# Three visits of P.V instead of two in the first three heads of a fused attention and GLU kernel

## The chip, the cores and the metric

The kernel runs on one core of a Trainium2 chip. The metric is the time of one execution on the device in microseconds (us), median of several runs. The kernel before takes 2607.92 us (three runs, 2605.91 to 2611.41).

## The reference

One sequence of 2048 tokens, width 576, 32 heads of 18 columns, and a gated feed-forward of width 4608, all in float32. Both halves read the same normalised input, and their results are multiplied.

```python
xn = _layernorm(x, axis=-1)
qkv = xn @ wqkv                                  # 576 -> 3 * 576
p = _softmax(einsum("bhqd,bhkd->bhqk", q, k) * (Dh ** -0.5))
s = einsum("bhqk,bhkd->bhqd", p, v) @ wo
h = einsum("bsd,df->bsf", xn, w_gate) * einsum("bsd,df->bsf", xn, w_up)
g = _silu(einsum("bsf,fd->bsd", h, w_down))
return x + s * g
```

## The kernel before, in words

There are three stages. First come the layer norm, the q, k and v projections and the first loads of the feed-forward's weights. The main stage then does the whole attention and the whole feed-forward together. A short end stage applies wo, multiplies and adds. Products keep float32 accuracy by splitting operands into a high and a low part, so a matmul of the feed-forward comes in three terms.

In the main stage TensorE (PE) is split into two halves of 64 rows each. Each half takes matmuls of its own, side by side with the other's. Five kinds of work are dealt to them:

- **A items** (`a_item`, L655): scores of 128 queries against 512 keys, only to find each row's maximum. They run on half 0 (head 0's on both). VectorE (DVE) reduces each (L657). 64 per head.
- **B items** (`b_item`, L707): the scores once more, transposed and with the maximum subtracted. They run on half 1. ScalarE (ACT) takes the exponential (L709) into a buffer `pt`. 64 per head, four for each block `t` of 128 keys; the ring of `pt` holds eight such blocks.
- **The up and gate products** (`gu_op`, L760): up on half 0, gate on half 1, 27 matmuls of 512 columns for each block of 128 hidden columns. ACT, DVE and GpSimd (POOL) evacuate and split the product.
- **The down product** (`down_op`, L811): groups of twelve matmuls of 288 columns, six on half 0 and then six on half 1 in the same PSUM bank. DVE adds the sum to its accumulator (L874), or ACT copies it out (L868) and POOL adds it (L838).
- **P.V** (`pv_group`, L718): probabilities times values. It is the one kind that uses all 128 rows, split into four column blocks of 32. It can therefore only run when both halves are through with what they were given. Such a turn is called a **visit**. ACT copies out the sum of a head's first visit (L722), and DVE adds the sum of each later one (L724).

No engine decides this order while it runs. The kernel writes it when it is built: `order` keeps a planned clock for each half and for the other engines, and at each step takes the next A or B item, the next feed-forward matmul, or a visit. A and B items are paced by a course (`a_goal`, `b_goal`) that is renewed every 32 items from the work that is left (`keep_course`). A visit is wanted when enough finished blocks are due, and it waits until the two planned clocks stand within 0.04 us of each other, or 2 us have passed (L1274 to L1281). How many blocks are enough is what `wanted` says. It shares what is left of a head evenly among the fewest visits of at most `MANY` = 8 blocks: 16 blocks make two visits of eight. Once all B items are done, one block is enough.

Weights are loaded by SP. In the first of four passes over the tokens they come from the inputs (`wraw`, `draw`), are split by ACT and POOL (L255, L256, L293, L294), used, and stored to `swg` and `swd` (L264, L301); the later passes load the split form back (L246, L285). SP also loads the stacks of q and k for the coming head (`load_stack`, L321). SP's queue stands in the order that the plan's times gave.

Of the kernel before, what the change touches and what calls it, by code (L numbers as in the profile page):

```python
# [41 lines left out]
def kernel(  # L42
# [594 lines left out]
    with ExitStack() as mid:  # L637
# [373 lines left out]
        LEAD, MOST, MANY = 16, 40, 8  # L1011
# [17 lines left out]
        due, jobs, rows_done = [], [], {}  # L1029
# [148 lines left out]
        def wanted():  # L1178

            if not due:  # L1180
                return 0
            if nb == TOTAL:
                return 1
            left = NT - due[0][1]
            return left // -(-left // MANY)

        upped, gated, downed = {}, {}, {}

# [67 lines left out]
        def order():  # L1256
# [5 lines left out]
            while going(0) or going(1) or na < TOTAL or nb < TOTAL or due or jobs or soon or pool_later:  # L1262
# [7 lines left out]
                if job and max(next_free("a"), next_free("b")) <= min(clk):  # L1270
                    rows(job)
                    continue
                need = wanted() if next_free("g") < 1e9 else 0
                if (need and len(due) >= need and due[need - 1][2] <= now  # L1274
                        or any(j[1] is finish for j in jobs) and nb == TOTAL and not due):
# [175 lines left out]
```

## Time and profile before

| | |
|---|---|
| median of three runs | 2607.92 us |
| the profiled execution, its own time | 2609.18 us |
| its span in the trace | 2606.7 us |
| first stage (to the first A item, at 195.63) | 195.6 us |
| main stage (to the end stage's first transpose, at 2534.15) | 2338.5 us |
| of it P.V, 64 visits of 7.07 us | 452.7 us |
| end stage | 72.5 us |
| PE, DVE, ACT, POOL busy, share of the span | 99%, 68%, 60%, 26% |

A row of the grouped view reads: source line, engine, operation, tile written <- tiles read, shape, count, then busy time, mean ns of one, and the engine's idle time ahead of these instructions with what ended it. PE's busy time is the union of both halves: PE counts as busy while one half works alone. In the timeline a row is a start, a duration, and the instructions merged into it; a matmul's duration is the time through the array, and the spacing of starts is what it costs its half.

### The profile page before, as it was taken

To read this page: it belongs to the slowest core of one execution; us is meant where nothing else is said; L and a number is where in the kernel's file an instruction comes from. 1 tells how busy PE (TensorE), PEld (TensorE's weight loads), DVE (VectorE), ACT (ScalarE), POOL (GpSimd) and SP (SyncE) were. 2 spreads that over 40 slices of the span, in tenths; PEclk is the share of its full clock that TensorE was granted. 3 is DMA by queue.
4 is the path that set the end of the run, shared out by engine and by line. 5 is a ranking of instruction groups with operands and counts; after the bars stand their busy time and mean duration, and the time that the engine had idled before them with its cause. 6 is when DMAs were issued, how large, how long until landed. Compare 5 with 4: busy or idle time off the path is not lost.

```text
span 2606.7 us, 59535 instructions
## 1 busy us (share of the span) xinstructions
PE 2593.6 (99%) x24504; PEld 2136.3 (82%) x24504; DVE 1774.3 (68%) x2950; ACT 1560.1 (60%) x3122; POOL 678.6 (26%) x704
## 2 busy tenths in 40 slices
PE   8999999999999999999999999999999999999999
PEld 7899878878887878878877887887878877888799
DVE  7208666767777777767777877776778777776136
ACT  4223666667766666766666666666666666667512
POOL 3114434434431222222211222212111222212015
PEclk9999999999999999999999999999999999999999
DMA  7799767676653445445545444443453354433266
GB/s 247 240 291 265 201 186 189 182 192 191 176 185 118 141 137 179 151 144 170 144 167 150 142 143 131 135 140 134 147 174 111 135 153 149 143 117 126 96 242 214
DMA packets 207696, 435.11 MB, mean 167 GB/s; under 512 B 83168, under 2 KB 132992, under 8 KB 177216
## 3 DMA queue, kind: packets, MB, share of 16 engines
q1 hardware_dynamic: 205264, 423.35, 53.1%
q0 software_dynamic: 2160, 7.96, 0.8%
q8 instruction: 192, 3.15, 0.5%
q14 instruction: 80, 0.66, 0.1%
HBM read 314.64 MB, written 111.35 MB: 163 GB/s over the span
## 4 chain that ended last, share of the span: by engine, by line
PE 99%; DVE 0%; DMA 0%; ACT 0%; issue 0%; DVEq 0%
PE pg L760 35%; PE pg L718 17%; PE pg L811 16%; PE pa L655 11%; PE pb L707 9%; PE pb L447 2%; PE pg L1403 2%; PE pg L504 2%; PE pa L447 2%; DMA wgu<-swg 0%; PE pb L1380 0%; PE pa L707 0%; PE pg L387 0%; PE pb L655 0%; DVE mx L657 0%; DVE st L344 0%
## 5 line engine op out<-in xcount | busy, mean ns | idle before, releaser
L657 DVE TENSOR_REDUCE mx<-pa 128x1 f32<-128x512 f32 x2016 | 1348.5, 687 | 364.8 <-PE pa L655 174.2
L709 ACT ACTIVATE pt<-pb 128x512 f32<-128x512 f32 x2006 | 1154.5, 603 | 481.4 <-PE pb L707 377.7
L760 PE MATMUL pg<-xc,wgu 64*128 64x512 f32 x7776 | 1433.8, 392 | 1.2 <-DMA wgu<-swg 1.1
L760 PEld LDWEIGHTS pg<-xc,wgu 64*128 64x128 f32 x7776 | 1066.2, 186 | 52.4 <-DMA wgu<-swg 1.3
L811 PE MATMUL pg<-wd,hs 64*128 64x288 f32 x6816 | 856.9, 293 | 0.0
L811 PEld LDWEIGHTS pg<-wd,hs 64*128 64x128 f32 x6816 | 797.2, 185 | 11.4 <-issue 1.7
L655 PE MATMUL pa<-whole,turning 54*128 54x512 f32 x1999 | 782.3, 398 | 0.7 <-DVE mx L657 0.7
L707 PE MATMUL pb<-whole,turning 56*128 56x512 f32 x1994 | 780.1, 398 | 0.0
L718 PE MATMUL pg<-pt,vt 128*32 128x512 f32 x4096 | 452.7, 594 | 0.0
L655 PEld LDWEIGHTS pa<-whole,turning 54*128 54x128 f32 x1999 | 363.6, 184 | 72.4 <-issue 50.5
L791 POOL TENSOR_TENSOR hs<-us,hs 128x512 fp32r<-128x512 f32 x144 | 185.9, 1291 | 876.0 <-ACT hs L778 666.0
L838 POOL TENSOR_TENSOR acc<-acc,st 128x288 f32<-128x288 f32 x291 | 234.3, 808 | 567.2 <-ACT st L868 356.9
L707 PEld LDWEIGHTS pb<-whole,turning 56*128 56x128 f32 x1994 | 362.9, 184 | 8.3 <-ACT pt L709 0.7
L718 PEld LDWEIGHTS pg<-pt,vt 128*32 128x32 f32 x4096 | 126.5, 110 | 285.2 <-issue 278.2
L724 DVE TENSOR_TENSOR oc<-oc,pg 128x512 f32<-128x512 f32 x32 | 22.0, 688 | 218.7 <-PE pg L718 218.7
L256 POOL TENSOR_TENSOR wgu<-wraw,wgu 128x384 fp32r<-128x384 f32 x108 | 108.2, 1018 | 211.4 <-ACT wgu L255 149.2
L722 ACT ACTIVATE oc<-pg 128x512 f32<-128x512 f32 x32 | 19.2, 599 | 228.2 <-PE pg L718 228.2
L874 DVE TENSOR_TENSOR acc<-acc,pg 128x288 f32<-128x288 f32 x254 | 113.8, 449 | 42.3 <-PE pg L811 38.8
L773 DVE TENSOR_TENSOR us<-pg,us 128x512 f32<-128x512 f32 x144 | 98.4, 683 | 59.9 <-PE pg L760 50.8
L868 ACT ACTIVATE st<-pg 128x288 f32<-128x288 f32 x291 | 120.3, 414 | 27.4 <-PE pg L811 19.8
L766 ACT ACTIVATE us<-pg 128x512 f32<-128x512 f32 x144 | 86.6, 601 | 71.4 <-PE pg L760 66.7
L778 ACT ACTIVATE hs<-us 128x512 fp32r<-128x512 f32 x144 | 91.2, 633 | 14.2 <-DVE us L773 13.9
(145 smaller groups left out, 1270.2 us busy)
## 6 DMA issues: line engine op xcount, KB each, us to landing
wgu<-swg SPq DMA_DIRECT2D x102, 1152.0 KB
wd<-swd SPq DMA_DIRECT2D x50, 1152.0 KB
swg<-wgu SPq DMA_DIRECT2D x36, 1152.0 KB
whole<-sqk SPq DMA_DIRECT2D x192, 144.0 KB
turning<-sqk SPq DMA_DIRECT2D x384, 72.0 KB
swd<-wd SPq DMA_DIRECT2D x18, 1152.0 KB
sqk<-hl SPq DMA_DIRECT2D x32, 512.0 KB
xc<-sx SPq DMA_DIRECT2D x24, 512.0 KB
```

Source lines behind the costliest of these rows:

```text
L256: nc.gpsimd.tensor_tensor(w[:, 9 + b:12 + b, :], raw[:, b:b + 3, :], w[:, b:b + 3, :].bitcast(FT), op=OP.subtract)
L655: nc.tensor.matmul(p, q[rows, t * 128:(t + 1) * 128], k[rows, c * 512:(c + 1) * 512], start=True, stop=True)
L657: nc.vector.tensor_reduce(mx[h][:, t, c:c + 1], p, axis=AX.X, op=OP.max)
L707: nc.tensor.matmul(p, k[rows, t * 128:(t + 1) * 128], q[rows, c * 512:(c + 1) * 512], start=True, stop=True)
L709: nc.scalar.activation(pt[t, c // 2][:, c % 2, :], p, AF.Exp, scale=scale)
L718: nc.tensor.matmul(p[32 * c:32 * c + 32, :], vt[h // 2][:, t, 6 * (h % 2):6 * (h % 2) + 32], pt[t, c // 2][:, c % 2, :], start=t == ts[0], ...
L760: nc.tensor.matmul(ps, gw[n][half[r], a, :], xg[i][half[r], e, :], start=k == 0, stop=k == len(TERMS) - 1)
L791: nc.gpsimd.tensor_tensor(hj[:, 1, :], h32, hj[:, 0, :].bitcast(FT), op=OP.subtract)
L811: op = nc.tensor.matmul(ps[:, 0:HALF], hs[u][half[r], j, a, s * 128:(s + 1) * 128], dw[u][half[r], j, e, i * HALF:(i + 1) * HALF], start=( ...
L838: nc.gpsimd.tensor_tensor(a, a, st, op=OP.add)
L868: nc.scalar.activation(st, ps[:, 0:HALF], AF.Copy)
L874: nc.vector.tensor_tensor(a, a, ps[:, 0:HALF], op=OP.add)
```

## The change

One expression in `wanted` changes. The head of the oldest due block decides: for heads 0, 1 and 2 a visit has at most six blocks, for the others at most eight as before.

```diff
@@ -1182,7 +1182,7 @@
             if nb == TOTAL:
                 return 1
             left = NT - due[0][1]
-            return left // -(-left // MANY)
+            return left // -(-left // (6 if due[0][0] < 3 else MANY))
```

With 16 blocks left this gives 16 // 3 = 5, then 11 // 2 = 5, then 6. As the plan is made step by step, everything behind the first such visit is dealt anew.

The order that comes of it: 67 visits instead of 64, of 5, 5, 6, 5, 5, 6, 5, 5, 6 blocks and then 58 of 8. PE has the same matmuls of each kind. DVE has 35 instead of 32 additions L724 and 270 instead of 254 L874; ACT has 275 instead of 291 L868, and POOL 275 instead of 291 L838. SP has the same transfers.

PE around the first visit (head 0), before:

```order
L655 MATMUL pa<-whole_1158,turning 128x512
L760 MATMUL pg<-xc,wgu 128x512
L811 MATMUL pg<-wd,hs 128x288 x2
L760 MATMUL pg<-xc,wgu 128x512 x6
L811 MATMUL pg<-wd,hs 128x288
L718 MATMUL pg<-pt,vt 32x512 x32
```

The same place in the changed kernel, 99 rows earlier:

```order
L811 MATMUL pg<-wd,hs 128x288 x3
L760 MATMUL pg<-xc,wgu 128x512
L655 MATMUL pa<-whole_1158,turning 128x512
L707 MATMUL pb<-whole_1157,turning 128x512
L811 MATMUL pg<-wd,hs 128x288 x5
L718 MATMUL pg<-pt,vt 32x512 x20
```

The first visit has five blocks of four matmuls in place of eight, and it stands earlier, with less work of the halves ahead of it.

PE in head 1, at its twelfth B item (the second L707 below), before. With buffer numbers the halves can be told: A items (L655) and the down group pg_4181 are half 0's, B items and the gate bank pg_4005 are half 1's, and pg_4156 is here still half 0's.

```order
L707 MATMUL pb_4167<-whole1_1158,turning_1155 128x512
L811 MATMUL pg_4156<-wd_3890,hs_3504 128x288 x2
L760 MATMUL pg_4005<-xc_1616,wgu_3731 128x512
L811 MATMUL pg_4156<-wd_3890,hs_3504 128x288 x2
L655 MATMUL pa_4178<-whole0_1157,turning_1155 128x512
L811 MATMUL pg_4181<-wd_3890,hs_3504 128x288 x3
L655 MATMUL pa_4191<-whole0_1157,turning_1155 128x512
L707 MATMUL pb_4195<-whole1_1158,turning_1155 128x512
```

The changed kernel around the same B item (here pb_4145; pg_3996 is the up bank of half 0, pg_4067 the gate bank of half 1):

```order
L655 MATMUL pa_4135<-whole0_1157,turning_1155 128x512
L707 MATMUL pb_4139<-whole1_1158,turning_1155 128x512
L760 MATMUL pg_3996<-xc_1616,wgu_3712 128x512
L760 MATMUL pg_4067<-xc_1466,wgu_3712 128x512
L760 MATMUL pg_3996<-xc_1616,wgu_3712 128x512
L707 MATMUL pb_4145<-whole1_1158,turning_1155 128x512
L655 MATMUL pa_4148<-whole0_1157,turning_1155 128x512
L760 MATMUL pg_4067<-xc_1616,wgu_3712 128x512
```

Before, seven matmuls of half 0 in a row (two L811, A, three L811, A) stand between two of half 1. In the changed kernel the halves alternate here, since other feed-forward work has come to this place.

SP's queue in the first pass, from six rows behind the maxima of head 1 (L693) on (a piece of the difference, lines with - before, with + of the change):

```order
-L301 DMA swd<-wd 128x2304
-L156 DMA draw<-in_B_w_down_dram 128x2x576
-L321 DMA turning<-sqk 18x1024 x3
-L264 DMA swg<-wgu 128x2304
-L149 DMA wraw<-in_B_w_up_dram 64x9x128
-L150 DMA wraw<-in_B_w_gate_dram 64x8x128
-L151 DMA wraw<-in_B_w_gate_dram 64x128
-L321 DMA whole_1157<-sqk 18x2048 x3
```

```order
+L321 DMA turning<-sqk 18x1024 x3
+L321 DMA whole_1157<-sqk 18x2048 x3
+L301 DMA swd<-wd 128x2304
+L156 DMA draw<-in_B_w_down_dram 128x2x576
```

The stacks for the next head (L321) now stand ahead of the store of `swd` and the load of `draw`, and two rounds of stores and loads of up and gate weights have moved behind them.

## The prediction

> **What bounds the kernel now.** I read the page's first part and its chain first, then whom PE waits for (us in total, times, longest), then the main stage as one window, then the group of P.V.
>
> ```profile
> PE 2593.6 (99%) x24504; PEld 2136.3 (82%) x24504; DVE 1774.3 (68%) x2950; ACT 1560.1 (60%) x3122; POOL 678.6 (26%) x704
> PE 99%; DVE 0%; DMA 0%; ACT 0%; issue 0%; DVEq 0%
> PE pg L406 <- DVE xn L355: 6.6, 2, 6.3
> PE pg L760 <- DMA wgu<-swg: 1.1, 1, 1.1
> PE pa L655 <- DVE mx L657: 0.7, 2, 0.4
> 195.63:2534.15 2338.52, 2336.42 (x22945) 1902.53 (x22944) 1659.44 (x2713) 1479.93 (x2928) 599.33 (x605) 1.00 0.52 157
> L718 PE MATMUL pg<-pt,vt 128*32 128x512 f32 x4096 | 452.7, 594 | 0.0
> ```
>
> PE is 99% busy and is 99% of the chain. In the main stage (the window row) it idles 2.1 us in 2338.5, at a granted clock of 1.00; the longest wait of the list, 6.6 us, lies in the first stage. So the bound is PE's order, and neither DVE nor a transfer. But busy here means that at least one half works. P.V takes 452.7 us; 2338.5 - 452.7 = **1885.8 us** are left for the two halves. What they have to do is counted, once a matmul's price is known:
>
> ```profile
> 2471.49 11.29 PE L760 MATMUL pg<-xc,wgu 64*128 64x512 f32 x97
> ...
> 2451.43 0.39 PE L760 MATMUL pg<-xc,wgu 64*128 64x512 f32 x1
> 2451.66 0.39 PE L707 MATMUL pb<-whole,turning 56*128 56x512 f32 x1
> 2451.90 0.39 PE L760 MATMUL pg<-xc,wgu 64*128 64x512 f32 x1
> 2452.13 0.39 PE L707 MATMUL pa<-whole,turning 56*128 56x512 f32 x1
> ...
> 2526.33 0.29 PE L811 MATMUL pg<-wdl,hs 64*128 64x288 f32 x1
> ...
> 2526.46 0.29 PE L811 MATMUL pg<-wdl,hs 64*128 64x288 f32 x1
> ...
> 2526.59 0.29 PE L811 MATMUL pg<-wdl,hs 64*128 64x288 f32 x1
> ```
>
> In the first row both halves work: 97 matmuls in 11.29 us, (11.29 - 0.39) / 96 = 0.114 us each, or 0.23 us for its half. In the next four one half works alone, and starts stand 0.23 us apart: the same price to that half, while the other half gains nothing. Both pieces count as busy. The last rows give 0.13 us (I use 0.132) for 288 columns. The order has 7776 + 4096 matmuls of 512 columns, 6912 of 288, and 64 small ones (0.06 us by my estimate): 3646.8 us, or 1823.4 us for each half if none ever stood alone. 62 us of the stage are thus something else: halves standing alone, and the ends of the stretches between visits.
>
> **How much stands alone.** PE takes its instructions in order. I walked down PE's rows with these prices: a matmul starts when its half is free, and not ahead of the row before it; a visit waits for both halves. Summed over its 65 stretches the order of before gives 1854.4 us, that is 31.0 us with one half alone. If only the balance of a stretch counted, and not the order in it, it would be the larger half's sum, 1841.7 us. The trace shows how strict the order is, at the place in head 1 that the second pair of listings above shows:
>
> ```profile
> 343.11 0.39 PE L760 MATMUL pg<-xc,wgu 64*128 64x512 f32 x1
> 343.21 0.42 PE L811 MATMUL pg<-wd,hs 64*128 64x288 f32 x2
> 343.48 0.39 PE L655 MATMUL pa<-whole,turning 54*128 54x512 f32 x1
> 343.71 0.42 PE L811 MATMUL pg<-wd,hs 64*128 64x288 f32 x2
> 343.89 0.50 PE L707 MATMUL pb<-whole,turning 56*128 56x512 f32 x1
> 343.98 0.29 PE L811 MATMUL pg<-wd,hs 64*128 64x288 f32 x1
> 344.11 0.39 PE L655 MATMUL pa<-whole,turning 54*128 54x512 f32 x1
> ```
>
> Half 1 has nothing between 343.11 and 343.89: 0.78 - 0.23 = 0.55 us lost. The strict walk loses 0.73 us there. The B item starts at 343.89, ahead of the A item at 344.11 that stands before it in the order. So three quarters of the strict loss is real here.
>
> **The change, step by step.**
>
> *Work that stands alone.* The same walk down the changed order gives 1846.4 us over 68 stretches, 23.0 us alone; by the larger half of each stretch it is 1838.0. So the change takes off 8.0 us by strict order and 3.7 by balance alone. The strict figure by parts: heads 0 to 7 (the first 128 blocks of P.V) go from 14.5 to 8.7, the next 45 stretches from 9.9 to 6.5, the last four stretches rise from 6.6 to 7.8. Most of it comes from the dealing anew. With three quarters of the way from balance to strict order: 3.7 + 0.75 x 4.3 = **-6.9 us**.
>
> The Trainium skill ("TensorE: Matmul & The Clock Gate", Part 3, "The mechanism") says that matmuls start and end strictly in program order. The rows above differ by one place, so the measurement decides; by the rule this term would be -8.0, and the time 2601.1, inside the forecast's own case.
>
> *Three more visits.* The P.V matmuls stay 4096 records of the trace (two for each matmul of the order), 7.07 us for the 64 of a full visit. What a visit adds is the end of one stretch and the start of the next. One stretch of before, from a visit's end to the next one's start, in which the halves hardly ever stand alone:
>
> ```profile
> L760 PE MATMUL pg<-xc,wgu 64*128 64x512 f32 x107 | 18.6, 391 | 0.0
> L707 PE MATMUL pb<-whole,turning 56*128 56x512 f32 x32 | 12.5, 396 | 0.0
> L655 PE MATMUL pa<-whole,turning 54*128 54x512 f32 x31 | 12.1, 396 | 0.0
> L811 PE MATMUL pg<-wd,hs 64*128 64x288 f32 x96 | 10.1, 292 | 0.0
> ...
> 1887.87:1914.15 26.28, 26.28 (x267) 23.98 (x266) 23.27 (x38) 21.06 (x40) 5.78 (x6) 1.00 0.45 144
> ...
> 1000.45 7.07 PE L718 MATMUL pg<-pt,vt 128*32 128x512 f32 x64
> 1007.45 0.50 PE L655 MATMUL pa<-whole,turning 54*128 54x512 f32 x1
> 1007.46 0.50 PE L707 MATMUL pb<-whole,turning 56*128 56x512 f32 x1
> 1007.79 0.39 PE L655 MATMUL pa<-whole,turning 54*128 54x512 f32 x1
> ...
> 297.80:329.71 31.91, 31.71 (x300) 28.41 (x300) 27.02 (x45) 27.91 (x58) 17.88 (x17) 1.00 0.74 225
> ```
>
> 170 matmuls at 0.23 and 96 at 0.132, over two halves, are 25.9 us; the stretch took 26.28, so 0.39 us for a boundary. Part of it is seen directly: behind the visit at 1000.45 the second A item starts 0.34 us after the first, 0.11 more than in the stream. The dearest early stretch (the last row) took 31.9 us where the walk has 30.9. Three boundaries: 0.3 us at least, 3.0 at most; I take 3 x 0.39 = **+1.2 us**, since the typical stretch is the nearest row.
>
> This is where a rule speaks against the change: the Trainium skill ("TensorEngine Tiling (Array Packing)", "Key Properties") says that a switch of tiling mode drains TensorE. Every visit is two switches, and the 0.39 us are what the trace shows of it.
>
> *The other engines.* Evacuations shift with the order:
>
> ```profile
> L724 DVE TENSOR_TENSOR oc<-oc,pg 128x512 f32<-128x512 f32 x32 | 22.0, 688 | 218.7 <-PE pg L718 218.7
> L874 DVE TENSOR_TENSOR acc<-acc,pg 128x288 f32<-128x288 f32 x254 | 113.8, 449 | 42.3 <-PE pg L811 38.8
> L868 ACT ACTIVATE st<-pg 128x288 f32<-128x288 f32 x291 | 120.3, 414 | 27.4 <-PE pg L811 19.8
> ```
>
> DVE gets 3 x 0.688 + 16 x 0.449 = 9.2 us more, ACT 16 x 0.414 = 6.6 less. DVE idles 679 us of the main stage, and PE's waits for it there are the 0.7 us above. I cost it at nothing. If that cover is gone, it is the three L724, each of which holds up the maxima behind it in DVE's queue, and through them an A bank: 2.1 us at most. Shorter visits return `pt` buffers sooner, which brings nothing while B items go by the course.
>
> *Sum.* -6.9 + 1.2 = **-5.7 us**. On the profiled execution's own 2609.18 us that is 2603.5. The median of the runs shown lies 1.26 us lower, at 2607.92, and the changed kernel will be told by a median too, so I give 2607.92 - 5.7 = **2602.2 us**.
>
> **Rivals.**
>
> *Given back at the boundaries.* If the extra ends of stretches cost like the early one above (3.0 us), and PE overtakes more often than in the one place that I looked at (-3.7), it is -0.7 us: 2607.2. For it: heads 0 to 2 lie where stretches cost most. Against it: most stretches lie near the 0.39.
>
> *Slower, by late weights.* SP's queue is in order, and the change deals anew the stores and loads of the first pass (third listing), where transfers are nearest to their limit:
>
> ```profile
> 194.90:290.70 95.80, 95.73 (x919) 91.15 (x917) 79.69 (x133) 45.33 (x93) 45.40 (x44) 1.00 0.94 257
> wgu<-swg SPq DMA_DIRECT2D x102, 1152.0 KB
> ```
>
> Here the DMA engines are 94% busy at 257 GB/s. A transfer of 1152 KB (1.18 MB) takes 4.6 us at that rate; a feed-forward block that has to wait for one in full holds up L760 and, behind it in PE's order, both halves. From three such waits on, -5.7 + 13.8 = +8.1, the kernel is slower: 2616.0. Against it: before, one wait of 1.1 us was all, and the plan spaces loads by its own queue.
>
> *More than the sum.* The stage has 1885.8 - 1854.4 - 65 x 0.39 = 6.1 us that neither the walk nor a boundary explains: small waits inside stretches, which the new order may or may not repeat. If all went: 2596.1.
>
> That the change doesn't do what it says is out: the order has its 67 visits.
>
> **How the numbers follow.** The forecast case has 0.72, with 3 us either way around -5.7 for waits inside stretches; given back 0.17; late weights 0.07; more than the sum 0.04. About 0.2%, or 5.2 us, is what a measurement of this kernel can tell from no change. The forecast lies just past that line, so I split its case 0.47 faster and 0.25 same. Faster: 0.47 + 0.04 = 0.51; same: 0.25 + 0.17 = 0.42; slower: 0.07. The range takes the cheapest and dearest sums, -3.7 + 3.0 + 2.1 = +1.4 (2609.3) at the top, and strict order with cheap boundaries, -8.0 + 0.3, with most of the unexplained waits gone at the bottom, -13 (2595). Late weights stay outside.
>
> **What would show it.** The first nine visits of the changed trace last 4.4, 4.4 and 5.3 us in turn. The main stage without P.V falls from 1885.8 to about 1880 us, more than half of it by the end of head 7. The short stretches of heads 0 to 2 exceed their walk by about 0.4 us each; if by 1 us, the first rival holds. PE's list of waits stays free of transfers above 1 us; a row of PE waiting for `wgu` or `wraw` by several us is the second rival. I would be wrong altogether if the stage fell and the end stage, 72.5 us, grew by as much.

## The result and the profile after

The changed kernel takes 2604.07 us in the median of 22 runs (2602.67 to 2606.09), the kernel before 2608.32 us beside it (22 runs, 2605.91 to 2611.51). The ratio is 0.9984, with a 95% interval from 0.9978 to 0.9989: 4.2 us faster, between 2.9 and 5.7. It is a small gain, clear of the noise and a little under the 0.2% line. The forecast was -5.7 us.

The profiled execution took 2604.09 us, with a span of 2602.3. First the page's busy times, then the main stage as a window, then whom PE waited for:

```profile
PE 2588.8 (99%) x24504; PEld 2130.8 (82%) x24504; DVE 1793.6 (69%) x2969; ACT 1551.9 (60%) x3106; POOL 665.3 (26%) x688
```

```profile
195.80:2529.81 2334.01, 2331.49 (x22945) 1897.01 (x22944) 1677.46 (x2732) 1471.54 (x2912) 586.30 (x589) 1.00 0.52 158
```

```profile
PE pg L406 <- DVE xn L355: 6.7, 2, 6.4
PE pa L686 <- DVE neg L673: 1.1, 2, 0.8
PE pa L655 <- DVE mx L657: 1.1, 3, 0.5
```

The main stage is 4.5 us shorter (2338.5 to 2334.0), and the end stage is the same (2602.3 - 2529.81 = 72.5). PE is as full as before. The one wait for a transfer is gone. The wait for DVE at L686, the small matmuls that bring a head's row of maxima into the stacks, has grown: before, the same list had 0.2 us for it, in one wait.

The groups that the change touches, and three visits with what follows the first (timeline):

```profile
L718 PE MATMUL pg<-pt,vt 128*32 128x512 f32 x4096 | 453.3, 594 | 0.0
...
L874 DVE TENSOR_TENSOR acc<-acc,pg 128x288 f32<-128x288 f32 x270 | 121.0, 449 | 37.2 <-PE pg L811 33.9 <-PE pg L760 0.8 <-PE pa L655 0.3
L868 ACT ACTIVATE st<-pg 128x288 f32<-128x288 f32 x275 | 113.7, 414 | 20.1 <-PE pg L811 15.5 <-PE pa L655 1.9
L724 DVE TENSOR_TENSOR oc<-oc,pg 128x512 f32<-128x512 f32 x35 | 24.1, 688 | 221.9 <-PE pg L718 221.9
```

```profile
276.46 4.50 PE L718 MATMUL pg<-pt,vt 128*32 128x512 f32 x40
280.89 0.50 PE L655 MATMUL pa<-whole,turning 54*128 54x512 f32 x1
280.90 0.50 PE L707 MATMUL pb<-whole,turning 56*128 56x512 f32 x1
281.23 0.39 PE L655 MATMUL pa<-whole,turning 54*128 54x512 f32 x1
...
328.42 5.36 PE L718 MATMUL pg<-pt,vt 128*32 128x512 f32 x48
...
815.26 7.08 PE L718 MATMUL pg<-pt,vt 128*32 128x512 f32 x64
```

Visits of five and six blocks take 4.50 and 5.36 us, and the first A items behind one again start 0.34 us apart. The last row closes head 7. It ends 626.5 us into the main stage; before, the visit that closes head 7 ends there 632.5 us in. So 6.0 us are won by then, and 1.5 are given back later.

The main stage can be taken apart by the prediction's own count. "Walk" is the sum down PE's order at 0.23 and 0.132 us, strictly in order. A boundary is 0.37 us, the median by which a stretch without a row of maxima exceeds its walk in either trace. The rest is what stays: waits inside stretches.

| | before | after | difference |
|---|---|---|---|
| P.V | 452.7 | 453.3 | +0.6 |
| walk | 1854.4 | 1846.4 | -8.0 |
| boundaries, 65 and 68 at 0.37 | 24.1 | 25.2 | +1.1 |
| rest | 7.3 | 9.1 | +1.8 |
| main stage | 2338.5 | 2334.0 | -4.5 |

The 0.37 is not the price of a visit alone. Part of it grows with the length of a stretch: in the kernel with four visits a head (below), whose stretches are half as long, the same median is 0.27. One reason may be that 0.23 is rounded (the starts of one half alone, from 2451.43 to 2452.13 in the prediction's rows, stand 0.233 us apart). By the price that the four-visit kernel gives, 0.15 us a visit in the halves, the boundaries rise by 0.5 instead of 1.1 and the rest by 2.4 instead of 1.8. The walk's difference is hardly touched by this, as both orders have the same matmuls.

The largest of the rest is seen in the timeline of the changed kernel, in head 27:

```profile
2203.66 0.39 PE L760 MATMUL pg<-xc,wgu 64*128 64x512 f32 x1
2204.82 0.29 PE L686 MATMUL pa<-identr,neg 64*128 64x64 f32 x1 [0.76 <-DVE neg L673]
2204.82 0.29 PE L686 MATMUL pb<-identr,neg 64*128 64x64 f32 x1
```

In brackets is PE's idle time and what ended it. L686 stands in PE's order at a moment when DVE has not written `neg` yet, and both halves wait behind it.

### The profile page after: what moved, and what is told of

The parts are those of the page before. It is cut to its first block, busy times and chain, and to the rows that moved or that the text cites. A ratio compares the mean times of both kernels' runs of the same rounds, so it can differ in the third digit from the quotient of the medians.

```text
span 2602.3 us, 59511 instructions
## 1 busy us (share of the span) xinstructions
PE 2588.8 (99%) x24504; PEld 2130.8 (82%) x24504; DVE 1793.6 (69%) x2969; ACT 1551.9 (60%) x3106; POOL 665.3 (26%) x688
## 4 chain that ended last, share of the span: by engine, by line
PE 98%; DVE 1%; ACT 0%; DMA 0%; issue 0%; POOL 0%; DVEq 0%; POOLq 0%
PE pg L760 35%; PE pg L718 17%; PE pg L811 16%; PE pa L655 11%; PE pb L707 8%; PE pb L447 2%; PE pg L1403 2%; PE pg L504 2%; PE pa L447 2%; DVE mx L657 1%; PE pa L707 0%; PE pb L1380 0%; PE pg L387 0%; DVE neg L673 0%; DVE us L773 0%; PE pb L655 0%
## 5 line engine op out<-in xcount | busy, mean ns | idle before, releaser
L657 DVE TENSOR_REDUCE mx<-pa 128x1 f32<-128x512 f32 x2016 | 1352.4, 687 | 343.4 <-PE pb L707 166.8
L760 PE MATMUL pg<-xc,wgu 64*128 64x512 f32 x7776 | 1418.5, 392 | 0.1
L811 PE MATMUL pg<-wd,hs 64*128 64x288 f32 x6816 | 839.3, 293 | 0.0
L811 PEld LDWEIGHTS pg<-wd,hs 64*128 64x128 f32 x6816 | 783.1, 185 | 9.9 <-DVE us L773 0.2
L655 PE MATMUL pa<-whole,turning 54*128 54x512 f32 x1999 | 780.7, 397 | 1.2 <-DVE mx L657 1.1
L707 PE MATMUL pb<-whole,turning 56*128 56x512 f32 x1993 | 779.8, 397 | 0.1
L718 PE MATMUL pg<-pt,vt 128*32 128x512 f32 x4096 | 453.3, 594 | 0.0
L655 PEld LDWEIGHTS pa<-whole,turning 54*128 54x128 f32 x1999 | 363.5, 184 | 77.3 <-issue 53.8
L707 PEld LDWEIGHTS pb<-whole,turning 56*128 56x128 f32 x1993 | 362.6, 184 | 6.4 <-ACT pt L709 0.7
L838 POOL TENSOR_TENSOR acc<-acc,st 128x288 f32<-128x288 f32 x275 | 221.6, 809 | 528.2 <-ACT st L868 349.3
L724 DVE TENSOR_TENSOR oc<-oc,pg 128x512 f32<-128x512 f32 x35 | 24.1, 688 | 221.9 <-PE pg L718 221.9
L874 DVE TENSOR_TENSOR acc<-acc,pg 128x288 f32<-128x288 f32 x270 | 121.0, 449 | 37.2 <-PE pg L811 33.9
L868 ACT ACTIVATE st<-pg 128x288 f32<-128x288 f32 x275 | 113.7, 414 | 20.1 <-PE pg L811 15.5
L778 ACT ACTIVATE hs<-us 128x512 fp32r<-128x512 f32 x144 | 90.8, 630 | 22.0 <-DVE us L773 21.7
```

The costliest lines, as they stand in the source:

```text
L655: nc.tensor.matmul(p, q[rows, t * 128:(t + 1) * 128], k[rows, c * 512:(c + 1) * 512], start=True, stop=True)
L657: nc.vector.tensor_reduce(mx[h][:, t, c:c + 1], p, axis=AX.X, op=OP.max)
L707: nc.tensor.matmul(p, k[rows, t * 128:(t + 1) * 128], q[rows, c * 512:(c + 1) * 512], start=True, stop=True)
L718: nc.tensor.matmul(p[32 * c:32 * c + 32, :], vt[h // 2][:, t, 6 * (h % 2):6 * (h % 2) + 32], pt[t, c // 2][:, c % 2, :], start=t == ts[0], ...
L760: nc.tensor.matmul(ps, gw[n][half[r], a, :], xg[i][half[r], e, :], start=k == 0, stop=k == len(TERMS) - 1)
L811: op = nc.tensor.matmul(ps[:, 0:HALF], hs[u][half[r], j, a, s * 128:(s + 1) * 128], dw[u][half[r], j, e, i * HALF:(i + 1) * HALF], start=( ...
```

## The experiments

The theory: the time follows the strict walk, plus about 0.36 us for each visit more, plus waits inside stretches that no count sees. The first rival: shorter visits help of themselves, for instance by keeping DVE and ACT fed. The second: only part of what stands alone is real, as the prediction had it. Below, ratios are against the kernel before, run beside each, and are given in us of 2608.

### The plan dealt anew, without a visit more

```diff
-EASE, TAIL, PACE, SKEW, PULL, FIRST = 1.0, 100, 1.005, 1.0, 3.0, 0.4
+EASE, TAIL, PACE, SKEW, PULL, FIRST = 1.0, 105, 1.005, 1.0, 3.0, 0.4
```

> Two visits in every head as before; only the constant TAIL of the course is 105 instead of 100, so that the plan is dealt anew without a visit more. The strict walk down PE's order gives 1846.9 us against 1854.4 before, the larger half of each stretch 1837.4 against 1841.7. Theory (time follows the strict walk plus 0.36 us for each visit more): -7.5 us, two either way for waits inside stretches. Strict order at three quarters, as in the prediction: -6.7. Balance alone: -4.3. Rival (the shorter and earlier visits of the first heads are what helps, by keeping DVE and ACT fed): no change, 0.

Measured: 2599.71 us against 2608.28, ratio 0.9965 (0.9952 to 0.9979): -9.1 us, between -12.5 and -5.5. The main stage as a window, and PE's waits in full:

```profile
194.48:2524.56 2330.08, 2329.80 (x22945) 1890.75 (x22945) 1657.57 (x2701) 1480.92 (x2940) 609.64 (x617) 1.00 0.52 158
```

```profile
PE pg L406 <- DVE xn L355: 6.7, 2, 6.4
PE pb L447 <- ACT xcx L408: 0.5, 1, 0.5
PE pa L686 <- DVE neg L673: 0.2, 1, 0.2
```

PE idles 0.3 us in the main stage. The rest of the table above is 6.4 us here. The gain is larger than the change's, with two visits in each head: the first rival, which forecast 0, falls. So does balance alone (-4.3); three quarters (-6.7) and strict order (-7.5) both lie in the interval. The kernel beats both others.

### More work alone

```diff
-FROM, STEP, WAITING = 54, 0, 1
+FROM, STEP, WAITING = 56, 0, 1
```

> Two visits in every head as before; FROM is 56 instead of 54, which lets the down products fall further behind and leaves one half alone far more often. Strict walk 1877.0 us against 1854.4 before, larger half of each stretch 1849.6 against 1841.7. Theory (strict walk): +22.6 us. Three quarters of the way from balance to strict order: +18.9. Balance alone: +7.9. Rival (visits are what matters): 0.

Measured: 2633.51 us against 2608.28, ratio 1.0095 (1.0081 to 1.0109): +24.8 us, between 21.1 and 28.4. The main stage:

```profile
195.20:2560.00 2364.80, 2359.91 (x22945) 1940.37 (x22944) 1667.64 (x2716) 1475.51 (x2925) 598.97 (x602) 1.00 0.51 156
```

It is 26.3 us longer, of which PE's idle time is only 2.8 (4.9 against 2.1): the other 23.5 us look like work, but in them one half stands alone. The strict +22.6 lies inside the interval; three quarters (+18.9) and balance alone (+7.9) lie below it. But the 2.8 us more of idle time are in the measured time and in none of these sums; with them three quarters comes to +21.7, which lies inside. So this run throws out balance alone, and does not settle the second rival.

The twelve traces together say more. I took each stretch between visits as one point, 854 in all (one with a long wait for a transfer, shown below, is left out), and fitted its time beyond the larger half's sum to what strict order adds there, with a constant, a term for a row of maxima and one for the stretch's length. Each us that strict order adds comes back as 0.90 us of time, between 0.76 and 0.99 if the twelve runs are drawn anew at random. So about nine tenths of the strict loss is real.

### Four visits in every head

```diff
-return left // -(-left // MANY)
+return left // -(-left // (4))
```

> Four visits of four blocks in every head (128 visits instead of 64). Strict walk 1846.6 us against 1854.4 before. Theory: -7.8 + 64 x 0.36 = +15.2 us. If a boundary costs 0.6 us, as the stretches with a row of maxima show it: +30.6. If visits cost nothing: -7.8. Rival (shorter visits help of themselves): faster than the change under study, below -4.

Measured: 2622.49 us against 2608.28, ratio 1.0053 (1.0039 to 1.0067): +13.8 us, between 10.2 and 17.5. The main stage as a window, and P.V's part of it:

```profile
194.82:2548.20 2353.38, 2351.95 (x22945) 1866.85 (x22944) 1705.78 (x2792) 1475.61 (x2913) 588.01 (x590) 1.00 0.52 156
```

```profile
194.82:2548.20 2353.38, 465.99 (x4096) 120.00 (x4096) 1.00 0.52 156
```

The main stage is 14.9 us longer while its walk is 7.8 shorter, so 64 visits cost 22.7 us, **0.355 us each**. Of that, 13.3 / 64 = 0.21 is in P.V itself (465.99 against 452.7), and 0.15 in the halves around it. By the interval of the measured time it is 0.28 to 0.40, if the waits inside stretches stayed as they were, which is not shown. A price of 0.6, and help from short visits, are both out.

### One head at a time, and three late heads

In `wanted`, `6 if due[0][0] < 3 else MANY` becomes, in turn:

```diff
+6 if due[0][0] == 2 else MANY
+6 if due[0][0] == 0 else MANY
+6 if 26 <= due[0][0] < 29 else MANY
```

> Only head 2 has three visits (65 visits). Strict walk 1849.1 us against 1854.4 before. Theory: -5.3 + 0.4 = -4.9 us, two either way. Balance alone: -3.1 + 0.4 = -2.7. Rival (visits help of themselves): a third of the change's -4.2, -1.4.

> Only head 0 has three visits (65 visits). Strict walk 1850.2 us against 1854.4 before. Theory: -4.2 + 0.4 = -3.8 us, two either way for waits inside stretches. Rival (a third of the change's -4.2 for each of the three heads): -1.4.

> The same edit put on heads 26, 27 and 28 instead of 0, 1 and 2: again 67 visits, nine of them short. Strict walk 1855.9 us against 1854.4 before. Theory (strict walk plus 0.36 us for each visit more): +1.5 + 1.1 = +2.6 us, two either way. Rival (shorter visits help of themselves, wherever they are): about -4, as in the change under study.

| | count | measured | interval | rest |
|---|---|---|---|---|
| head 2 alone | -4.9 | -1.6 | -3.9 to +0.8 | 11.7 |
| head 0 alone | -3.8 | -0.8 | -2.9 to +1.6 | 9.7 |
| heads 26 to 28 | +2.6 | +1.6 | -0.8 to +3.9 | 5.5 |
| the change | -6.9 | -4.2 | -5.7 to -2.9 | 9.1 |

The same edit in three late heads does not make the kernel faster by 4 us, which the first rival needs. For head 2 and head 0 the count missed by 3 us, and a third of the change's gain for each head fits both better; these two runs alone would not exclude the first rival, as the others do. The loss lies in the rest: for head 2 alone it is 4.4 us above the kernel before's 7.3. Among PE's own waits there is one for weights:

```profile
PE pg L760 <- DMA wgu<-swg: 1.5, 1, 1.5
```

The kernel before has the same wait with 1.1 us, so this explains 0.4; where the other 4 us went is not shown. So the count is right to about 3 us, and small gains can be given back whole.

### DVE's maxima over half the columns

Both kernels with their orders untouched:

```diff
-nc.vector.tensor_reduce(mx[h][:, t, c:c + 1], p, axis=AX.X, op=OP.max)
+nc.vector.tensor_reduce(mx[h][:, t, c:c + 1], p[:, 0:256], axis=AX.X, op=OP.max)
...
-nc.scalar.activation(pt[t, c // 2][:, c % 2, :], p, AF.Exp, scale=scale)
+nc.scalar.activation(pt[t, c // 2][:, c % 2, :], p, AF.Exp, scale=0.05 * scale)
```

> The changed kernel with its order untouched on every engine, but DVE's maxima (L657) read 256 of 512 columns, and the exponential's scale is 0.05 of what it was so that all stays finite: the maxima over the other half of the keys and the true softmax are left out. DVE then never runs late. Theory (the change's walk is worth -8.0 and its boundaries +1.1, and the rest was given back to A items and rows of maxima that wait for DVE): this kernel stands 6.9 us below the next one. Rival (what was given back went to something else, transfers or the boundaries): it stands 4.2 below, as the change does.

> The kernel before with the same two edits (maxima over 256 columns, exponential at 0.05 of its scale), its order untouched. Theory: what waits for DVE goes, 1 to 4 us below the kernel before; the wait of about 1 us for a transfer of weights stays. Rival (PE never waits for DVE to a measurable sum): 0.

Measured: the changed kernel so 2595.69 us, ratio 0.9953 (0.9939 to 0.9966), -12.3 us; the kernel before so 2600.44, ratio 0.997 (0.9959 to 0.9982), -7.8 us (-10.7 to -4.7). The waits of PE's weight loads show what went. First the kernel before, then the changed kernel, then the kernel before with half maxima (there the group of L657 too, 687 ns before, 422 now):

```profile
PEld pa L655 <- DVE mx L657: 6.4, 23, 0.9
PEld pa L686 <- DVE neg L673: 1.8, 6, 0.4
```

```profile
PEld pa L655 <- DVE mx L657: 5.1, 17, 0.8
PEld pa L686 <- DVE neg L673: 3.6, 8, 1.2
```

```profile
PEld pa L655 <- DVE mx L657: 0.6, 1, 0.6
```

```profile
L657 DVE TENSOR_REDUCE mx<-pa 128x1 f32<-128x256 f32 x2016 | 839.4, 422 | 784.0 <-PE pa L655 529.6 <-PE pb L707 194.9 <-PE pg L760 27.6
```

A items that waited for their bank, 23 times and 6.4 us together, wait once. The wait for a transfer, which I expected to stay, is not in this execution, though the order is the same; whether it left with the faster DVE, or differs from one execution to the next, one trace of each kernel cannot tell. So DVE's lateness is worth some 6 to 8 us to both kernels: their main stages are 7.0 and 7.8 us shorter, the first with the 1.1 us of that transfer in it. The rest falls from 7.3 to 0.4 us before and from 9.1 to 1.3 after.

But the two kernels stand 4.8 us apart by their medians, not the 6.9 that I expected: the theory's last clause, that the change's gain was given back to late maxima, does not hold as it was put. By the profiles their main stages are 5.3 us apart (2331.5 and 2326.2), against 4.5 with the whole maxima: of the 1.8 us of rest, 0.8 goes with DVE's lateness and 1.0 stays. The lists above point the same way: their two rows sum to 8.2 us before and 8.7 after. One piece of what stays is a lag of 0.8 us at L686 between the visits of head 28 (from 2261.01 to 2261.87 in the changed one's timeline), where the row of maxima stands too early in the order even for a DVE this fast. The intervals of these two runs are too wide to settle more.

### Two plans picked by the count

Two visits in every head. The first has LEAD 15, TAIL 104, SKEW 1.1, PULL 4.0, FIRST 0.45; the second TAIL 107, SKEW 1.1, PULL 4.0, QUICK 0.7.

> Two visits in every head; five constants of the plan moved (LEAD 15, TAIL 104, SKEW 1.1, PULL 4.0, FIRST 0.45) to the lowest strict walk of the plans that were built: 1846.2 us against 1854.4 before, larger half of each stretch 1835.9 against 1841.7. Theory: -8.2 us, and between 0 and 3 us given back to A items and rows of maxima that wait for DVE, so -8.2 to -5.2. Rival (the shorter visits help of themselves): 0.

> Two visits in every head; four constants of the plan moved otherwise (TAIL 107, SKEW 1.1, PULL 4.0, QUICK 0.7). Strict walk 1847.2 us against 1854.4 before, larger half of each stretch 1835.6 against 1841.7. Theory: -7.2 us, and between 0 and 3 us given back, so -7.2 to -4.2. Rival (the shorter visits help of themselves): 0.

Measured: the first 2600.74 us, ratio 0.9973 (0.9962 to 0.9985), -7.0 us (-9.9 to -3.9), as counted. The second 2609.05 us, ratio 1.0005 (0.9996 to 1.0013), +1.3 us (-1.0 to +3.4): the count missed by 8 us. Its timeline, soon after the last visit, says why:

```profile
2469.94 6.98 PE L760 MATMUL pg<-xc,wgu 64*128 64x512 f32 x50
2480.03 8.71 PE L811 MATMUL pg<-wd,hs 64*128 64x288 f32 x86 [3.10 <-DMA wd<-swd]
```

PE stands idle for 3.1 us for one load of down weights. SP issued it at 2471.36, behind the stores of the last heads' output (L743), and two loads of `wgu` right behind it, at 2471.89; it landed 8.5 us after its issue. In the kernel before, the corresponding load (2472.24) has 5.6 us until the next `wgu` load is issued, and PE does not wait. The idle time is not all that it costs, as three windows show: the wait, what follows it, and 4 us from 2484.70 on.

```profile
2476.92:2480.03 3.11, 0.01 (x2) 0.03 (x1) 0.69 (x1) 0.63 (x1) 0.00 (x0) 0.64 1.00 414
2480.03:2484.30 4.27, 4.27 (x27) 4.27 (x29) 0.00 (x0) 0.00 (x0) 1.27 (x1) 0.50 0.76 315
2484.70:2488.70 4.00, 4.00 (x61) 4.00 (x61) 2.14 (x6) 0.00 (x0) 0.00 (x0) 1.00 0.00 0
```

The third number from the end is the granted clock. It is 0.50 behind the wait, where PE gets through 27 matmuls in 4.27 us, and 1.00 again later, with 61 in 4.00. At the later pace 27 take 1.8 us, so 2.5 us more are lost there. In none of the other eleven traces is the clock of the main stage below 1.00, and in none does PE stand idle there for more than 1.5 us at a time; that the idle time brought the clock down is likely from this one case, not shown. The whole stretch takes 5.1 us more than its walk; in the kernel before it took 0.8 less. The eleven runs of this kernel all list a mean clock of 0.998 or 0.999 and those of the kernel before 1.0, so the loss comes with the plan and not by chance. This is the prediction's second rival, late weights, in another plan: the count of PE's order does not know the loads.

## Why the prediction was right, and where its sum was off

- **The bound** was read rightly: PE's order. Orders with another amount of work alone and the same visits moved the time by -9.1 and +24.8 us.
- **Work that stands alone, -6.9.** The mechanism was right and the size was cut a little too far. Balance alone is out by two runs, and the traces together give nine tenths of the strict loss, which makes this term -7.6 (-7.0 to -8.0 by the fit's range). "Three quarters of the strict loss is real here" was read from one place and carried to the whole stage. A start that overtakes by one place there hardly shortens the whole; the rule of the Trainium skill ("TensorE: Matmul & The Clock Gate", "The mechanism"), which single starts do not follow, comes nearer to the sum. The prediction's 0.06 us for each of the 64 small matmuls stands in no row; it is the same in every order and cancels.
- **Three more visits, +1.2.** The size was right: 0.355 us each in the four-visit run, 1.1 us for three. Its parts were not: the prediction put all of it into the halves and held P.V constant, but P.V itself took 0.6 us more, 0.21 a visit. The drain that the Trainium skill names for a switch of mode ("TensorEngine Tiling (Array Packing)", "Key Properties") is inside these 0.355 us; no run shows it by itself.
- **The other engines, nothing.** The reading behind this failed. I read PE's waits for DVE as 0.7 us, from the list of PE's own idle time. The weight loads' list had 6.4 us, and fast maxima gave 7.8 (4.7 to 10.7). In a stage where one half goes on working, a half that waits hardly shows as PE idle. The term itself, what the change adds to these waits, was off by less: 0.8 us went with fast maxima, inside the 2.1 that the prediction allowed. The heads with three visits have none of the added rest: what their stretches have beyond walk and boundary is 2.2 us before and 1.3 after.
- **The sum, -5.7.** Measured -4.2 (-5.7 to -2.9). On the profiled executions it was -5.1 in their own times (2609.18 to 2604.09). That it came so near is in part luck. Two errors, about 0.7 us too little gained and some 2 us too little given back, partly cancel, and the rest could have moved further: in the seven other orders with DVE untouched, without the four-visit one, it moved by -1.8 to +8.1 us.
- **The rivals.** Given back at the boundaries: no, the short stretches of heads 0 to 2 exceed their walk by 0.3 to 0.7 us. Late weights: not here, but seen elsewhere. More than the sum: no.

What stays open: 1.0 us of the rest that the changed order has more (1.6 by the lower price of a boundary), spread over many stretches, and why the count missed head 2 and head 0 by 3 us.

## What to carry to other kernels

Where an engine works in two halves, its busy share does not tell whether one half stands alone: count that by walking down the order with each half's spacing, and calibrate the remainder on the old trace. An edit to a rule of a planner deals everything behind it anew; try the same deal without the edit before crediting the edit. Such a count was good to 3 us in 2608 for most plans here, and blind to late loads, to the clock behind them and to another engine's lateness.

## What the runs showed of the hardware

- Full-array P.V costs 0.107 us a record (two to a matmul) and 0.21 us a visit: 7.07 us for 64 records, and 465.99 / 128 = 3.64 for 32.
- One wait for a load of 1152 KB cost 3.1 us of idle PE and 5.9 us of its stretch: behind it the granted clock stood at 0.50 for 4.3 us.
- The first stage is the same code in all these kernels, and took 193.8 to 195.8 us in the profiled executions: 2 us of scatter that no change explains.
